# Stacked float32r scores for batch 1, and weights decoded in the tile they land in, in an attention and two-MoE-layer kernel

## The chip, the cores and the metric

One core of one Trainium2 chip runs the whole program; seven cores of the chip are idle. The metric is the device time of one execution in microseconds, the median of several runs. TensorE is called PE here, VectorE DVE, ScalarE ACT, GpSimd POOL, and SyncE, which issues most of the DMAs, SP.

## The reference

The inputs are q, k, v of shape 4 x 8 x 576 x 64 (batch, heads, positions, head size), s of shape 4 x 8 x 576, and five weight matrices that arrive as 64-bit numbers. What is computed, cut to what matters:

```python
scores = scale * q @ k.T
cum = cumsum(maximum(s, 0), axis=-1)
bias = -(cum[:, :, :, None] - cum[:, :, None, :])
scores = where(causal, -1e9, scores + minimum(bias, 0))
x = softmax(scores) @ v            # then 2304 tokens x 512
x = ((x @ w_a) * (x @ w_b)) @ w_out        # 512 -> 1536 -> 512
h = x @ w_in                               # 512 -> 2048
out = (maximum(h, 0) + alpha * minimum(h, 0)) @ w_out2
```

## The kernel before

The 2304 tokens are worked through in five blocks, four of 512 and one of 256. A batch has 576 positions, so block b holds the last 64 positions of batch b-1 and the first 512 (or fewer) of batch b. For each block the two feed-forward layers run on PE (`ffn`, line 1094), and the attention that the next block needs is woven between their matmuls as a list of steps (`attention`, line 895): block 0's matmuls carry the attention of batch 1 (and the tail of batch 0), block 1's that of batch 2, block 2's that of batch 3. The attention of batch 0 comes first, by itself (`first_attention`, line 850). From its pass `i >= FROM_STEPS` on, that lead-in also takes three steps per pass off block 0's list (line 890), six in all: the scores of the tail (`s4`), the scores of heads 0 and 1 of batch 1 for query rows 0 to 255 (`s01`), the next loads, two calls of `both` (biases), and the scores for rows 256 to 383 (`s23`).

The feed-forward layers work in three single-precision products per matrix product: every operand is split into a float32r high part and low part, and `mm3` (lines 1087 to 1089; 1198 to 1200 for the last layer) multiplies high by high, high by low and low by high. A weight tile is 128 x 512; a block uses 68 of them, `NW`, each for 12 matmuls. The split of a weight into `wh` (a copy on ACT) and `wl` (a subtraction on DVE or POOL, line 284) takes place once per block and weight, into six pairs of buffers.

Weights come as 64-bit floats, 512 KB a tile. `load_w` (line 1006) has two ways. The first way loads the 64-bit tile into one of five `raw` tiles (RAW = 5), and `decode` (line 982) turns it into float32: ACT writes the exponent part into `top` (line 987), DVE merges the rest (the SCALAR_TENSOR_TENSOR at line 278). The second way, `again` (line 1038), loads a pair of already decoded tiles from a scratch tensor `w_d` in HBM, 512 KB for two weights. In block 0 every weight goes the first way and is decoded into one of four `w32` tiles; the raw tile is free as soon as the decoding is done. Two thirds of them (46, those whose pair number is not 1 modulo 3) are stored to `w_d` from the w32 tile by a DMA that ACT issues (line 1060); the w32 tile is free when the split and the store are done. The remaining third (22) is not stored in block 0: it is loaded as 64 bits again in block 1, decoded there in place in its raw tile, and stored. From block 2 on all weights come from `w_d`.

Scores (`q_k`, line 494) have two forms. Batches below `STACK` (0 and 1) multiply q and k in plain float32 with a contraction of 64, two heads side by side in the two halves of the array (line 528). Batches 2 and 3 take the stacked form: k is split into high and low parts, q's high and low parts lie one above the other in 128 rows (`stack`, line 435: two copies and two subtractions per head, and two loads of 512 KB per pair of heads instead of two of 256 KB), and each head needs two float32r matmuls with a contraction of 128 (line 502). The stack's tiles kh and qs take two w32 slots each head; `of_stack` opens only when the last weight of block 0 has got its w32 tile.

Biases also have two forms. Batches below `SUMS_PE` (0 and 1) add the running sums on PE, by two float32r matmuls per head and group of rows (lines 518 and 522), and the causal mask comes in with the reduction that moves the scores out of PSUM. For batches 2 and 3 `biases` (line 542) loads each head's running sums to all partitions (`cb`, a broadcast DMA of 256 KB, `load_sums`), forms the bias on DVE or ACT (lines 571 and 575) and masks the diagonal on POOL (line 581).

The order of instructions on each engine is made while the program is built. `Order` holds a rough clock of each engine; every vector operation is placed on the engine that can start or end it first, in order of start and then of due time, where loads of weights have 10 us of slack and splits 5 us. An operation that DVE's second port and POOL share counts as holding both ("port", line 86). DMAs of SP go out in the order of the program, and a DMA that waits for a buffer holds up those behind it. At most ten weights beyond the one in use are asked for (AHEAD = 10, line 1073). The ring of PSUM banks for attention has two banks in the blocks; a step needs both free.

The planner's weave is one line (1232): steps are spread evenly over the block's 272 groups of matmuls.

```python
want = min(len(steps), (i + 1) * len(steps) * FASTER / total)
```

Of the kernel before, what the change touches and what calls it, by code (L numbers as in the profile page):

```python
# [11 lines left out]
I32 = mybir.dt.int32  # L12
# [9 lines left out]
P = 128  # L22
# [33 lines left out]
LATE, LATE_0 = 1000.0, 1300.0  # L56
SL_LOAD, SL_PARTS, SL_QK, SL_BIAS = 10000.0, 5000.0, 5000.0, 2500.0

SUMS_PE = 2

STACK = 2

TURN, SPACE = 1, 5


FROM_WEIGHTS, AHEAD, FROM_LEAD, FROM_STEPS, STEPS = 2, 10, 3, 4, 3


FASTER, BEFORE = 1.06, 6
# [129 lines left out]
def attention_two_moe_kernel(  # L199
# [16 lines left out]
    NW = w64.shape[0]  # L216
    NF1 = (NW - 2 * NF2) // 3
    WN = 512
# [10 lines left out]
    wraw = ctx.enter_context(tc.tile_pool(name="wraw", bufs=1))  # L229
# [6 lines left out]
    W32, RAW, KQ, VB, CB, KL, TOPS = 4, 5, 3, 4, 3, 2, 2  # L236
# [4 lines left out]
    of_raw, of_kq, of_w32, of_w, of_vb, of_t, of_pb, of_c0, of_c1, of_kl = (  # L241
        Slots(n) for n in (RAW, KQ, W32, 6, VB, 4, 1, CB, 2, 0)
    )
    of_stack = Slots(0)

    ctx.enter_context(
        tc.manual_schedule(
# [3 lines left out]
    run = Order()  # L251
# [598 lines left out]
    def first_attention():  # L850
        nonlocal ahead
        s_sb = work.tile([BH, S], F32, name="s_sb", tag="z4")
        nc.scalar.activation(alpha_sb[:, 0:1], ident[:, 0:1], AF.Exp)
        nc.sync.dma_start(s_sb, s)
        for i in range(2):
            load_kq(0, i, 0)
        run.now = 2000.0
        run.pump()
        running_sums(s_sb)
        run.now = 5000.0  # L860
        for rs in ((0, 1), (2,)):
            both(0, 0, rs)
        for i in range(HP + 2):
            if i + 2 < HP:
                load_kq(0, i + 2, 0)
            if i < HP:
                load_v(0, i, 0)
                both(0, i, (3,))
                s01(0, i)
                if i + 1 < HP:  # L870
                    both(0, i + 1, (0, 1))
            if 0 <= i - 2:
                av(0, i - 2, 0)
            if i < HP:
                s23(0, i, 2)
                if i + 1 < HP:
                    both(0, i + 1, (2,))
                s23(0, i, 3)
            if i == FROM_WEIGHTS:
                nc.sync.dma_start(alpha_sb, alpha)  # L880
                ahead = AHEAD
                prefetch()
            if i == FROM_LEAD:
                for f, args in plan[0][0]:
                    f(*args)
            if 0 <= i - 1 < HP:
                for c in range(3):
                    for j in range(2):
                        turn(0, 2 * (i - 1) + j, c)
            if i >= FROM_STEPS:  # L890
                for f, args in plan[0][1][:STEPS]:
                    f(*args)
                del plan[0][1][:STEPS]

    def attention(blk):

# [109 lines left out]
    def load_w(n):  # L1006

        i = n % NW
        postponed = i // 2 % 3 == 1
        new = n < NW or (n < 2 * NW and postponed)  # L1010
        kept = new and postponed == (n >= NW)
        got = []

        def acquire():

            if n:
                yield turns[n - 1]
            yield fetched
            yield of_w

        def first():
            yield of_raw
            r = w64p.tile([P, 2 * WN + 2], I32, name="raw", tag="raw", bufs=RAW)
            yield from dma(r.bitcast(U16)[:, 1:1 + 4 * WN], w64[i].bitcast(U16))
            if n < NW:
                yield of_w32
                w = wraw.tile([P, WN], I32, name="w32", tag="w32", bufs=W32)
                if n == NW - 1:
                    for j in range(2):
                        run.give(of_stack, run.t)  # L1030
            else:
                w = r[:, 0:WN]
            source.append(w)
            yield from decode(n, r, w)
            if n < NW:
                run.give(of_raw, run.t)

        def again():
            if i % 2 == 0:
                pairs[i] = run.spawn(load_pair(i))  # L1040
            yield pairs[i - i % 2]
            source.append(pairs[i - i % 2, "w"][:, i % 2, :])

        def parts():
            yield turns[n]
            h = wsp.tile([P, WN], F32R, name="wh", tag="wh")
            l = wsp.tile([P, WN], F32R, name="wl", tag="wl")
            got.extend((h, l))
            yield from split(f32(source[0]) if new else source[0], h, l)
            if kept:  # L1050
                run.spawn(keep(stored), run.t)
            elif new:
                run.give(of_w32, run.t)
            elif i % 2:
                run.give(of_raw, run.t)

        def store():
            yield fetched
            yield {"act": 330}, 700
            nc.scalar.dma_start(w_d[i].bitcast(I32), source[0])  # L1060
            yield {"dma": P * WN / 90}, 900

        def keep(stored):
            yield stored
            run.give(of_w32 if n < NW else of_raw, run.t)

        source = []
        fetched = run.spawn(first() if new else again(), slack=SL_LOAD)
        stored = run.spawn(store()) if kept else None
        turns[n] = run.spawn(acquire())  # L1070
        return got, run.spawn(parts(), slack=SL_PARTS)

    def prefetch():
# [225 lines left out]
```

## Time and profile before

| | us |
|---|---|
| median of 3 runs | 1002.03 |
| lowest and highest of the runs | 998.98, 1002.17 |
| the profiled execution | 998.65 |
| its span, first to last instruction | 996.9 |
| PE busy in the span | 977.4 |
| DVE, ACT, POOL busy | 699.0, 566.8, 251.2 |
| mean granted TensorE clock | 0.998 |

The span is 1.75 us shorter than the profiled execution's own time. PE's busy time is a union of records whose ends are modelled; the start of one matmul to the start of the next tells more.

### The profile page before, as it was taken

How to read it: one execution, taken by the hardware profiler on the slowest of the kernel's cores; microseconds unless marked ns; L12 is line 12 of the kernel's file. 1: busy time of each engine (PE TensorE's matmuls, PEld its weight loads, DVE VectorE, ACT ScalarE, POOL GpSimd, SP SyncE). 2: the span in 40 equal slices, each digit the busy share in tenths (PEclk: the TensorE clock that was granted, in tenths of full speed). 3: DMA queues.
4: the chain of work that ended last, by engine and by line, in shares of the span. 5: the costliest groups of instructions: out<-in, count | busy, mean ns of one | idle time of the engine just before them, and what ended most of it. 6: DMA issues, size and time to landing. Idle time of an engine off the chain costs nothing.

```text
span 996.9 us, 16282 instructions
## 1 busy us (share of the span) xinstructions
PE 977.4 (98%) x5381; PEld 808.2 (81%) x5381; DVE 699.0 (70%) x1612; ACT 566.8 (57%) x1154; POOL 251.2 (25%) x308
## 2 busy tenths in 40 slices
PE   6989999999999999999999999999999999999998
PEld 5667777778888888788888888888888888889997
DVE  7888877886779788977477777954444474546685
ACT  5866766776655566555554446644433354446664
POOL 2131221441224342432142214522010032210032
PEclk9999999999999999999999999999999999999999
DMA  6599999899688979568387665563542523317551
GB/s 181 188 286 315 349 324 324 295 340 305 237 279 266 317 245 317 192 223 278 103 263 252 188 232 166 185 191 107 190 161 84 171 84 119 132 59 245 185 181 51
DMA packets 149332, 214.62 MB, mean 215 GB/s; under 512 B 36288, under 2 KB 80320, under 8 KB 149248
## 3 DMA queue, kind: packets, MB, share of 16 engines
q1 hardware_dynamic: 139456, 195.76, 61.4%
q10 hardware_dynamic: 9792, 17.83, 4.8%
q8 instruction: 42, 0.69, 0.3%
q14 instruction: 42, 0.34, 0.1%
HBM read 169.95 MB, written 43.59 MB: 214 GB/s over the span
## 4 chain that ended last, share of the span: by engine, by line
PE 91%; DVE 3%; issue 2%; DMA 2%; ACT 1%; POOL 0%; SPq 0%; POOLq 0%; DVEq 0%; ACTq 0%
PE bank L1087 21%; PE bank L1088 21%; PE bank L1089 21%; PE bank L1198 7%; PE bank L1199 6%; PE bank L1200 6%; PE bank L766 2%; PE bank L502 2%; PE bank L706 1%; PE bank L528 1%; PE bank L827 1%; DMA raw<-in_w_dram 1%; DVE z L278 1%; PE bank L518 1%; ACT z L262 0%
## 5 line engine op out<-in xcount | busy, mean ns | idle before, releaser
L1087 PE MATMUL bank<-xh,wh 128*128 128x512 f32 (+1 forms) x800 | 298.6, 373 | 2.3 <-DVE g L278 2.3
L1088 PE MATMUL bank<-xl,wh 128*128 128x512 f32 (+1 forms) x800 | 294.7, 368 | 0.1
L1089 PE MATMUL bank<-xh,wl 128*128 128x512 f32 (+1 forms) x800 | 294.5, 368 | 0.0
L270 ACT ACTIVATE wh<-raw 128x512 fp32r<-128x512 f32 x267 | 166.8, 626 | 106.2 <-PE bank L1088 62.7
L284 POOL TENSOR_TENSOR wl<-raw,wh 128x512 fp32r<-128x512 f32 x83 | 110.5, 1332 | 360.4 <-ACT wh L270 297.3
L284 DVE TENSOR_TENSOR wl<-raw,wh 128x512 fp32r<-128x512 f32 x189 | 132.7, 703 | 92.5 <-ACT wh L270 87.5
L1087 PEld LDWEIGHTS bank<-xh,wh 128*128 128x128 f32 x800 | 150.8, 188 | 32.9 <-issue 4.8
L1088 PEld LDWEIGHTS bank<-xl,wh 128*128 128x128 f32 x800 | 150.8, 189 | 25.5 <-DVE xl L278 0.5
L1089 PEld LDWEIGHTS bank<-xh,wl 128*128 128x128 f32 x800 | 150.8, 188 | 25.4
L270 ACT ACTIVATE gh<-g 128x512 fp32r<-128x512 f32 (+1 forms) x140 | 82.1, 587 | 65.2 <-DVE g L278 62.8
L284 DVE TENSOR_TENSOR gl<-g,gh 128x512 fp32r<-128x512 f32 (+1 forms) x127 | 86.8, 683 | 38.2 <-ACT gh L270 36.2
L1198 PE MATMUL bank<-wh,gh 128*128 128x512 f32 x288 | 113.5, 394 | 0.0
L1199 PE MATMUL bank<-wl,gh 128*128 128x512 f32 x288 | 112.3, 390 | 0.0
L1200 PE MATMUL bank<-wh,gl 128*128 128x512 f32 x288 | 112.1, 389 | 0.0
L262 ACT ACTIVATE z<-z,mn 128x128 f32<-128x128 f32 (+4 forms) x144 | 82.8, 576 | 43.4 <-DVE mn L278 42.2
L1087 PE MATMUL bank<-gh,wh 128*128 128x512 f32 (+1 forms) x240 | 89.7, 374 | 0.0
L1088 PE MATMUL bank<-gl,wh 128*128 128x512 f32 (+1 forms) x240 | 88.7, 370 | 0.3 <-DVE gl L284 0.3
L1089 PE MATMUL bank<-gh,wl 128*128 128x512 f32 (+1 forms) x240 | 88.3, 368 | 0.0
L262 ACT ACTIVATE m<-bank 128x512 f32<-128x512 f32 (+1 forms) x80 | 44.1, 552 | 64.0 <-PE bank L1089 63.6
L987 ACT ACTIVATE top<-raw 128x512 f16<-128x512 bf16 x90 | 69.5, 785 | 17.1 <-DMA raw<-in_w_dram 16.2
L289 DVE TENSOR_SCALAR m<-m,alpha_sb 128x512 f32<-128x512 f32 (+1 forms) x70 | 34.8, 497 | 50.1 <-ACT m L262 49.2
L270 ACT ACTIVATE a_sb<-bank 128x512 f32<-128x512 f32 (+1 forms) x60 | 33.0, 549 | 60.4 <-PE bank L1089 58.5
(91 smaller groups left out, 1397.0 us busy)
## 6 DMA issues: line engine op xcount, KB each, us to landing
raw<-w_d SPq DMA_DIRECT2D x125, 512.0 KB, 4.3
raw<-in_w_dram SPq DMA_DIRECT2D x90, 512.0 KB, 5.8
w_d<-w ACTq DMA_DIRECT2D x46, 256.0 KB, 5.4
zd<-zt SPq DMA_DIRECT2D x48, 192.0 KB, 4.0
pt<-zd SPq DMA_DIRECT2D x48, 192.0 KB, 4.2
kq<-in_kq_a_dram SPq DMA_DIRECT2D x16, 512.0 KB, 6.3
vb<-in_v_dram SPq DMA_DIRECT2D x112, 64.0 KB, 4.1
zd<-zt SPq DMA_DIRECT2D x24, 256.0 KB, 3.6
```

The source lines that it names most:

```text
L262: nc.scalar.activation(o, i, func, **k)
L270: nc.scalar.activation(o, i, AF.Copy, scale=by)
L284: (nc.gpsimd if eng == "pool" else nc.vector).tensor_tensor(o, i0, i1, op=ALU.subtract)
L289: (nc.gpsimd if eng == "pool" else nc.vector).tensor_scalar(o, i, s0, s1, op0=ALU.mult, op1=ALU.mult)
L502: nc.tensor.matmul(d, qs[:, r * P:n], k[:, 0:n], start=i == 0, stop=i == 1)
L987: nc.scalar.activation(top.bitcast(F16).rearrange("p (n t) -> p n t", t=2)[:, :, 1], r.bitcast(BF16)[:, 4:4 + 4 * WN].rearrange("p (n t) - ...
L1087: nc.tensor.matmul(o, wh, ih, start=first, stop=False)
L1088: nc.tensor.matmul(o, wh, il, start=False, stop=False)
L1089: nc.tensor.matmul(o, wl, ih, start=False, stop=last)
L1198: nc.tensor.matmul(acc[t], gh[:, c], wh, start=first, stop=False)
L1199: nc.tensor.matmul(acc[t], gh[:, c], wl, start=False, stop=False)
L1200: nc.tensor.matmul(acc[t], gl[:, c], wh, start=False, stop=last)
```

## The change

Four things change. `SUMS_PE` and `STACK` fall from 2 to 1, so that batch 1 takes the stacked scores and the biases of the vector engines, as batches 2 and 3 do. The lead-in no longer takes six steps off block 0's list. The weights of block 0 are decoded in their raw tile, as the late third was; the raw tile is held until the weight is split and, where it is stored, until the store has landed. And the store is spread: a weight is decoded from 64 bits up to the block that equals its pair number modulo 3 and stored there, so that blocks 0, 1 and 2 (the first three) decode 68, 44 and 22 weights and store 24, 22 and 22. `of_stack` starts with two slots, and w32 tiles now serve the stack alone.

```diff
-SUMS_PE = 2
-STACK = 2
+SUMS_PE = 1
+STACK = 1
...
-FROM_WEIGHTS, AHEAD, FROM_LEAD, FROM_STEPS, STEPS = 2, 10, 3, 4, 3
+FROM_WEIGHTS, AHEAD, FROM_LEAD = 2, 10, 3
...
-    of_stack = Slots(0)
+    of_stack = Slots(2)
...
-            if i >= FROM_STEPS:
-                for f, args in plan[0][1][:STEPS]:
-                    f(*args)
-                del plan[0][1][:STEPS]
...
     def load_w(n):
         i = n % NW
-        postponed = i // 2 % 3 == 1
-        new = n < NW or (n < 2 * NW and postponed)
-        kept = new and postponed == (n >= NW)
+        new, kept = n // NW <= i // 2 % 3, n // NW == i // 2 % 3
...
             yield from dma(r.bitcast(U16)[:, 1:1 + 4 * WN], w64[i].bitcast(U16))
-            if n < NW:
-                yield of_w32
-                w = wraw.tile([P, WN], I32, name="w32", tag="w32", bufs=W32)
-                if n == NW - 1:
-                    for j in range(2):
-                        run.give(of_stack, run.t)
-            else:
-                w = r[:, 0:WN]
-            source.append(w)
-            yield from decode(n, r, w)
-            if n < NW:
-                run.give(of_raw, run.t)
+            source.append(r[:, 0:WN])
+            yield from decode(n, r, source[0])
...
             if kept:
                 run.spawn(keep(stored), run.t)
-            elif new:
-                run.give(of_w32, run.t)
-            elif i % 2:
+            elif new or i % 2:
                 run.give(of_raw, run.t)
...
         def keep(stored):
             yield stored
-            run.give(of_w32 if n < NW else of_raw, run.t)
+            run.give(of_raw, run.t)
```

## Rows read from the trace of the kernel before

**Rows 1.** The page's chain that ended last, by engine.

```profile
PE 91%; DVE 3%; issue 2%; DMA 2%; ACT 1%; POOL 0%; SPq 0%; POOLq 0%; DVEq 0%; ACTq 0%
```

**Rows 2.** Blocks 0, 1, 2: length, then busy us of PE, PEld, DVE, ACT, POOL.

```profile
56.20:275.80 219.60, 217.61 (x1175) 172.97 (x1174) 174.12 (x381) 149.82 (x292) 57.79 (x63) 1.00 0.92 306
275.80:490.50 214.70, 212.37 (x1137) 176.22 (x1136) 168.24 (x392) 124.91 (x257) 70.70 (x87) 1.00 0.77 248
490.50:702.50 212.00, 212.00 (x1137) 176.40 (x1136) 151.50 (x367) 110.23 (x233) 63.29 (x79) 1.00 0.62 196
```

**Rows 3.** Timeline of PE: a matmul ahead of and behind batch 1's scores (start, length).

```profile
79.50 0.39 PE L1089 MATMUL bank<-xh,wl 128*128 128x512 f32 x1
...
81.70 0.39 PE L1089 MATMUL bank<-xh,wl 128*128 128x512 f32 x1
...
112.09 0.39 PE L1089 MATMUL bank<-gh,wl 128*128 128x512 f32 x1
...
114.47 0.40 PE L1089 MATMUL bank<-gh,wl 128*128 128x512 f32 x1
```

**Rows 4.** The same around batch 2's stacked scores, in block 1.

```profile
280.66 0.39 PE L1089 MATMUL bank<-xh,wl 128*128 128x512 f32 x1
...
282.27 0.39 PE L1089 MATMUL bank<-xh,wl 128*128 128x512 f32 x1
...
302.07 0.39 PE L1089 MATMUL bank<-xh,wl 128*128 128x512 f32 x1
...
303.66 0.39 PE L1089 MATMUL bank<-xh,wl 128*128 128x512 f32 x1
```

**Rows 5.** Timeline of PE in the lead-in's last two passes, with idle time and releaser.

```profile
41.56 2.31 PE L773 MATMUL bank<-pt,vb 128*64 128x512 f32 x6
...
46.34 2.40 PE L733 MATMUL bank<-ident,z 128*128 128x128 f32 x20
...
51.68 0.37 PE L528 MATMUL bank<-kq 64*128 64x128 f32 x1 [1.20 <-DMA kq<-in_kq_a_dram]
...
52.76 2.37 PE L773 MATMUL bank<-pt,vb 128*64 128x512 f32 x16
...
58.93 0.97 PE L518 MATMUL bank<-cums,rows 64*128 64x512 f32 x2 [1.72 <-DVE mn L278]
```

**Rows 6.** PE's waits from 60 us on (total, times, longest), its largest.

```profile
PE bank L1087 <- DVE g L278: 2.3, 1, 2.3
```

**Rows 7.** Groups by line and shape over the whole run: the decoding's two operations.

```profile
L987 ACT ACTIVATE top<-raw 128x512 f16<-128x512 bf16 x90 | 69.5, 785 | 17.1 <-DMA raw<-in_w_dram 16.2 <-DMA cb<-cum_d 0.5
...
L278 DVE SCALAR_TENSOR_TENSOR raw<-raw,top 128x512 int32<-128x512 int32 x22 | 16.2, 750 | 3.4 <-ACT top L987 3.4
```

**Rows 8.** The busiest stretch of 40 us in block 1 (columns as in Rows 2).

```profile
396.00:436.00 40.00, 37.67 (x217) 31.08 (x216) 33.55 (x85) 25.15 (x55) 16.95 (x22) 1.00 0.67 217
```

**Rows 9.** Groups: the softmax scaling on DVE in two widths, and POOL's diagonal mask.

```profile
L289 DVE TENSOR_SCALAR z<-z,sm 128x512 f32<-128x512 f32 x28 | 16.4, 606 | 0.5
...
L289 DVE TENSOR_SCALAR z<-z,sm 128x128 f32<-128x128 f32 x20 | 10.0, 511 | 0.2
...
L581 POOL TENSOR_SCALAR_AFFINE_SELECT z<-z 128x256 f32<-128x256 f32 x16 | 9.9, 635 | 13.0 <-DVE z L571 10.5 <-ACT z L575 2.4
```

**Rows 10.** SP's own waits from 60 to 271 us: total, times, longest.

```profile
SPq L295 <- DVE w L278: 21.9, 18, 3.8
```

**Rows 11.** SP's timeline in block 0: the first and the last of nine raw loads.

```profile
184.55 1.50 SPq L295 DMA_DIRECT2D raw<-in_w_dram  x2
...
211.22 6.17 SPq L295 DMA_DIRECT2D raw<-in_w_dram  x4
```

**Rows 12.** Groups by line and shape: the two operations of a weight's split.

```profile
L270 ACT ACTIVATE wh<-w 128x512 fp32r<-128x512 f32 x67 | 41.6, 628 | 25.0 <-DVE w L278 9.1 <-PE bank L1088 5.0 <-PE bank L1089 2.3
...
L284 POOL TENSOR_TENSOR wl<-w,wh 128x512 fp32r<-128x512 f32 x31 | 41.2, 1329 | 100.2 <-ACT wh L270 58.3 <-DVE g L278 20.4 <-DVE m L289 8.0
```

**Rows 13.** DMA issues from 60 to 271 us: stores of block 0 (KB, us to landing).

```profile
w_d<-w ACTq DMA_DIRECT2D x43, 256.0 KB, 5.5
```

## The prediction, written before the change was run

> **What bounds the kernel now.** I read the chain of waits first: 91% of it is PE [rows 1], so time comes off where PE does less or waits less. The table of busy times by block says how much room the other engines have [rows 2]: in block 0 PE is busy 217.6 of 219.6 us, DVE 174.1 (79%), ACT 149.8 (68%), POOL 57.8; in block 1 DVE 168.2 of 214.7 (78%), ACT 124.9. DVE is the next engine. PE's timeline shows batch 1's scores between feed-forward matmuls [rows 3] and batch 2's stacked scores in block 1 [rows 4]; there the reader measures from the start of one matmul to the start of another, since the ends are modelled. The lead-in shows where PE waits today [rows 5], and PE's waits show that after 60 us there is only one of weight, 2.3 us for a DVE result in block 1 [rows 6].
>
> **The change, part by part.**
>
> *Scores.* For two heads, query rows 0 to 255: from the matmul ahead to the third one behind took 81.70 - 79.50 = 2.20 us in the old form [rows 3] and 282.27 - 280.66 = 1.61 us in the stacked form [rows 4], 0.59 us less. For query rows 384 to 511: 2.38 against 1.59, 0.79 less. The group between (query rows 256 to 383) I take at the mean, 0.69. So 2.07 us per pair of heads, and four pairs: 8.3 us of PE's time, on the path. Bounds: all groups like the smaller, 3 x 4 x 0.59 = 7.1; all like the larger, 9.5. Those numbers hold the sums' matmuls and the switching between forms, because the stretch ends at ordinary matmuls.
>
> *The six steps moved out of the lead-in.* Their matmuls are still done, in block 0. With them go two waits: 1.20 us for a kq load and 1.72 us for a reduction that had to free a bank [rows 5]. But they stood between the last transposes and the last attention product of the lead-in, whose input is copied out of PSUM by ACT in that time. How long that takes uncovered is shown one pass earlier: the product ran from 41.56 to 46.34, 4.78 us, where the covered one took 2.37 [rows 5], so 2.4 us come back. Net -0.5; bounds -2.9 (ACT copies in time) and +1.9 (the 2.4 come back, half of the two old waits remain or recur as a wait for weights: 2.4 - 0.5; nothing in the trace excludes that). SP has the moved loads later in its queue, behind weights; I cost that at nothing, covered by the matmuls between one step and the next; without that cover it is another wait of 1.2 us.
>
> *Vector work of block 0.* After the change block 0 is what block 1 is today, with 68 decodings in place of 22. That gives its load without guessing at each stack and bias: 46 decodings at 0.750 us on DVE and 0.785 us on ACT [rows 7] on top of block 1's rows [rows 2]: DVE 168.2 + 34.5 = 203 us, ACT 124.9 + 36.1 = 161 us, in a block that PE would finish in 219.6 - 8.3 = 211 us. DVE at 96% is too much to be left there; the planner gives a subtraction to whichever of DVE and POOL starts first, and POOL has two thirds of its time free. Today's busiest 40 us of block 1 (DVE 33.55, 84%) hold the one stall of 2.3 us [rows 6, 8]. Blocks above that load should have more. For block 0 I take one; none is the lower end; one in each of five stretches of 40 us, 11.7 us, the upper.
>
> *Blocks 1 and 2.* Each gets 22 more decodings: DVE +16.5, ACT +17.3 us, so block 1 stands at 185 of 215 us (86%), block 2 at 168 of 212 (79%). Block 2 then is where block 1 is now. For both together I take half a stall more, 1.2 us; bounds -2.3 (the present one is not met again) and +4.7 (two).
>
> *DMA.* Block 0 drops 22 stores (5.6 MB) and gains eight broadcasts and larger kq loads (4.1 MB); block 2 gains 22 stores where DMA is 62% busy [rows 2]. Nothing on the path, and covered by the weights' lead; without it, see the raw tiles below.
>
> **Sum.** -8.3 - 0.5 + 2.3 + 1.2 = -5.3 us. The profiled execution took 998.65 us (span 996.9, 1.75 around it), 3.4 below the median of 1002.03. I set the difference against the median: 996.7 us. A measurement of this kernel can tell about 0.3%, 3 us, from no change.
>
> **The rivals.**
>
> *The vector engines become the bound (no gain).* For it: DVE at 203 of 211 us, and POOL as an outlet that costs DVE time. The softmax scaling of 128 columns takes 511 ns on DVE, that of 512 columns 606 [rows 9]: a quarter of the work at 84% of the time, so much of the short one must be waiting, and it has no input that another engine could still owe it. The eight heads of batch 1 add masks on POOL, some 0.635 us for the first two row groups alone [rows 9], 5.1 us for eight heads. The Trainium skill (SBUF — State Buffer, "Who interferes with whom") says that DVE and GpSimd share a port pair as an exclusive lock, held for a whole instruction while the other engine fully blocks; by that rule each mask and each subtraction moved to POOL takes its length from DVE, and the two rows agree with it. Against it: there is no PE wait in block 0 at 79%, and decodings and splits can be late, the softmax not. Price: five stalls of 2.3 in block 0 and two in block 1 in place of my one and a half, +12.6 -> 1009 at its worst; half of that, the likelier depth, gives 1003.
>
> *Five raw tiles become the bound (slower).* Place: block 0. Today a raw tile is free when it is decoded, and even so SP stood 18 times, 21.9 us, waiting for just that [rows 10]. Between 184.55 and 211.22 us eight loads went out (two at the first row, six between), one per 3.33 us [rows 11], so that each of five tiles came round in 16.7 us. The change holds it longer: by the split, 0.63 + 1.33 us [rows 12] with POOL doing the subtraction, or, in 24 of 68, by the store's 5.5 us [rows 13]. That is 44/68 x 2.0 + 24/68 x 5.5 = 3.2 us, 19.9 us a round, 4.0 us a weight, against 211/68 = 3.1 that PE asks for. If this holds in half of the block, 34 weights are 0.9 us late each, 31 us; six pairs of split weights cover up to 6 x 3.1 = 19 us; 12 us reach PE. From 996.7 that is 1009. It decides where a round takes more than 5 x 3.1 = 15.5 us. Against it: the 16.7 contains waits of a queue that was well ahead, and SP's waits moved no PE time; and the planner, which sees the longer hold, orders the decoding accordingly.
>
> *Nothing else is late (faster still).* POOL takes enough of DVE's work, and the only stall of today is not met again: -8.3 - 0.5 - 2.3 gives 991. For it: the late work is all of the kind that can wait, and the rest of block 1 runs at 78% of DVE without a stall. Against it: its busiest stretch stalled at 84% [rows 6, 8], and block 0 will be above that on the mean.
>
> That the stacked form waits for its own preparation (copies and subtractions that begin only when the pair before is through) is a smaller one: at 1.2 us per pair, as the kq wait, it would add 4.8 and give 1001.5. In block 1 those matmuls stand in rows without idle time [rows 4], so I give it little.
>
> **How the numbers follow.** Forecast (one to two new stalls) 0.45; the vector engines 0.22; the raw tiles 0.20; nothing late 0.10; late stacks 0.03. Of the forecast, 0.40 lies beyond 3 us on the fast side and 0.05 within; of the vector case 0.14 within, 0.06 slower, 0.02 faster; of the raw tiles 0.17 slower, 0.03 within; nothing late is faster, late stacks are within. Faster 0.52, same 0.25, slower 0.23. The range runs from 989 (nothing late, and the lead-in at its lower end, 991 - 2.4) to 1010, the raw tiles in half of block 0 with an uncertain microsecond; about one in ten lies outside on the slow side, where the whole block would be held up, and less than that on the other. The likeliest case by itself: 993 to 1000.
>
> **What would show it.** The scores of batch 1 as L502-like rows at 0.9, 0.7 and 0.9 us per pair, in block 0; no wait for kq in the lead-in, and an attention product of some 4.8 us ahead of the first feed-forward matmul; 134 decodings; block 0 shorter by 5 to 8 us, blocks 1 and 2 longer by 0 to 3, and blocks 3 and 4 the same. DVE above 88% in block 0, with PE's waits naming g or mn. Wrong would be: PE waiting for wl or wh in block 0, and SP waiting for the store or the split ahead of raw loads (raw tiles); PE's waits above 10 us in blocks 0 and 1 with DVE named (vector engines); a block 0 that is no shorter although no wait shows, which would mean that the stacked form costs more there than in block 1.

## The result, and the profile after

The changed kernel takes 1010.07 us (median of 6 runs, 1008.51 to 1015.48) against 1001.9 for the kernel before beside it (6 runs): ratio 1.0093, 95% interval 1.0066 to 1.0119. It is 8.2 us slower where 5.3 us less were forecast. The profiled execution took 1008.51, with a span of 1006.7, 9.8 more than before.

First the page's chain that ended last, by engine [rows 1 before], and one of its groups [rows 7]:

```profile
PE 71%; DMA 12%; DVE 6%; issue 5%; ACT 3%; POOL 1%; SPq 1%; ACTq 0%; POOLq 0%; DVEq 0%
...
L983 ACT ACTIVATE top<-raw 128x512 f16<-128x512 bf16 x134 | 103.6, 786 | 55.3 <-DMA raw<-in_w_dram 53.5
```

PE has fallen from 91% to 71% of the chain, and DMA has risen from 2 to 12%. ACT's decoding, 134 times in place of 90, was idle 53.5 us for raw loads (16.2 before [rows 7]). Then the busy times by block, with the columns of [rows 2]; the row of a block begins at its first feed-forward matmul and ends at that of the next:

```profile
50.40:282.70 232.30, 219.97 (x1138) 177.68 (x1138) 185.45 (x412) 169.42 (x337) 73.62 (x92) 0.99 0.87 289
282.70:496.00 213.30, 212.75 (x1138) 176.08 (x1137) 178.22 (x407) 138.78 (x280) 81.96 (x90) 1.00 0.85 280
496.00:712.40 216.40, 214.09 (x1138) 177.49 (x1136) 163.71 (x384) 120.87 (x249) 71.42 (x86) 0.99 0.73 240
```

So the lead-in ends 5.8 us earlier (50.4 against 56.2), block 0 is 12.8 us longer (232.3 against 219.5), block 1 is 1.4 shorter, block 2 is 4.4 longer, and blocks 3 and 4 are unchanged at 192.9 and 97.6. But for rounding, that adds up to the span's +9.8. The DMA engines had no more to move: in block 0 they were busy 0.92 of the time at 306 GB/s before [rows 2], and 0.87 at 289 now. PE is idle 12.3 us of block 0 (2.0 before [rows 2]), while DVE has 47 us free. PE's waits from 50.4 us on, the largest (in total, times, longest):

```profile
PE bank L1071 <- DVE wl L284: 3.4, 2, 3.0
PE bank L1180 <- ACT gh L270: 3.3, 2, 2.2
PE bank L502 <- DVE mn L278: 2.3, 2, 1.8
PE bank L1069 <- ACT wh L270: 1.7, 2, 1.3
```

Weights are waited for (wl, wh), and with them gh, which ACT makes in program order behind the decoding; the two waits for mn lie in blocks 1 and 2. What the loads waited for is in SP's own waits in block 0:

```profile
SPq L295 <- DMA w_d<-raw: 41.3, 15, 6.0
SPq L295 <- DMA raw<-in_w_dram: 17.4, 18, 3.3
...
SPq L295 <- DVE wl L284: 14.5, 12, 5.1
```

Stores hold SP for 41.3 us, and splits (wl) for 14.5. SP waited for stores in the kernel before as well, in its block 0:

```profile
SPq L295 <- DMA w_d<-w: 24.6, 16, 4.9
```

One piece of the chain of waits shows how that reaches PE (start, length, what):

```profile
257.37 5.81 DMA raw<-in_w_dram
...
263.26 0.80 ACT top L983
...
266.64 0.65 DVE raw L278
...
267.32 5.15 DMA w_d<-raw
...
272.52 3.94 DMA raw<-in_w_dram
...
276.54 0.79 ACT top L983
...
277.96 0.70 DVE gl L284
...
278.70 0.76 PE bank L1182
```

A raw tile is decoded and its store takes 5.15 us. Only then does SP load the next weight; ACT's next decoding stands waiting for that, and what is queued behind it is late: gh, then gl, then the matmul. Taken over the weights 12 to 67 of block 0, from the records of the traces: a raw load was issued 16.0 us after its weight was asked for (4.3 before), counted from the first matmul of the weight ten places ahead of it, and a split was ready 4.0 us before its matmul (12.3 before). Two thirds of the lead are gone.

The stacked scores did what they should. PE's timeline in block 0, one matmul ahead of each of the three groups of a pair of heads and the third one behind it [rows 3, 4]:

```profile
195.93 0.39 PE L1071 MATMUL bank<-xh,wl 128*128 128x512 f32 x1
...
197.54 0.39 PE L1182 MATMUL bank<-wh,gl 128*128 128x512 f32 x1
...
204.35 0.39 PE L1182 MATMUL bank<-wh,gl 128*128 128x512 f32 x1
...
205.76 0.39 PE L1182 MATMUL bank<-wh,gl 128*128 128x512 f32 x1
...
219.80 0.39 PE L1182 MATMUL bank<-wh,gl 128*128 128x512 f32 x1
...
221.38 0.39 PE L1071 MATMUL bank<-xh,wl 128*128 128x512 f32 x1
```

1.61, 1.41 and 1.58 us, where the kernel before took 2.20, 2.07 and 2.38: 2.05 per pair, 8.2 in all four if they are alike. (This is the fourth pair; the first two took 1.99 and 1.88 us for their first group.)

### The profile page after: what moved, and what is told of

The parts are those of the page before. It is cut to its first block, busy times and chain, and to the rows that moved or that the text cites. A ratio compares the mean times of both kernels' runs of the same rounds, so it can differ in the third digit from the quotient of the medians.

```text
span 1006.7 us, 16432 instructions
## 1 busy us (share of the span) xinstructions
PE 977.1 (97%) x5317; PEld 809.6 (80%) x5317; DVE 732.3 (73%) x1666; ACT 610.4 (61%) x1240; POOL 286.4 (28%) x344
## 4 chain that ended last, share of the span: by engine, by line
PE 71%; DMA 12%; DVE 6%; issue 5%; ACT 3%; POOL 1%; SPq 1%; ACTq 0%; POOLq 0%; DVEq 0%
PE bank L1069 16%; PE bank L1070 16%; PE bank L1071 16%; PE bank L1182 5%; PE bank L1180 5%; PE bank L1181 5%; DMA raw<-in_w_dram 5%; DMA zd<-zt 3%; DMA w_d<-raw 2%; PE bank L502 2%; PE bank L766 2%; DMA cb<-cum_d 1%; PE bank L706 1%; ACT z L262 1%; DVE raw L278 1%
## 5 line engine op out<-in xcount | busy, mean ns | idle before, releaser
L284 POOL TENSOR_TENSOR wl<-raw,wh 128x512 fp32r<-128x512 f32 x121 | 161.7, 1340 | 395.3 <-ACT wh L270 303.4
L270 ACT ACTIVATE wh<-raw 128x512 fp32r<-128x512 f32 x335 | 207.9, 625 | 108.0 <-PE bank L1070 44.5
L284 DVE TENSOR_TENSOR wl<-raw,wh 128x512 fp32r<-128x512 f32 x219 | 152.5, 698 | 90.3 <-ACT wh L270 84.5
L983 ACT ACTIVATE top<-raw 128x512 f16<-128x512 bf16 x134 | 103.6, 786 | 55.3 <-DMA raw<-in_w_dram 53.5
L278 DVE SCALAR_TENSOR_TENSOR raw<-raw,top 128x512 int32<-128x512 int32 x134 | 98.6, 746 | 27.7 <-ACT top L983 24.5
L581 POOL TENSOR_SCALAR_AFFINE_SELECT z<-z 128x128 f32<-128x128 f32 (+2 forms) x104 | 53.3, 520 | 140.8 <-DVE z L571 81.7
L262 ACT ACTIVATE m<-bank 128x512 f32<-128x512 f32 (+1 forms) x80 | 43.9, 548 | 51.9 <-PE bank L1071 50.5
```

The source lines that it names most:

```text
L262: nc.scalar.activation(o, i, func, **k)
L270: nc.scalar.activation(o, i, AF.Copy, scale=by)
L278: f(*args, **k)
L284: (nc.gpsimd if eng == "pool" else nc.vector).tensor_tensor(o, i0, i1, op=ALU.subtract)
L581: nc.gpsimd.affine_select(d, d, pattern=pattern, base=0, channel_multiplier=1, compare_op=ALU.is_ge, fill=MASKED,)
L983: nc.scalar.activation(top.bitcast(F16).rearrange("p (n t) -> p n t", t=2)[:, :, 1], r.bitcast(BF16)[:, 4:4 + 4 * WN].rearrange("p (n t) - ...
```

## The experiments

Labels are shortened in the text to their first part. "Start" is the time of block 0's first feed-forward matmul, the end of the lead-in. Lengths are those of the profiled execution, from a block's first feed-forward matmul to the next block's, and to the last matmul for block 4. Each ratio is against runs of the kernel before beside it. "Stores" counts the weights stored in blocks 0 to 3. Each kernel is the changed one with the edit named; from `e13` on, `top` is taken from a list of free tiles instead of by the weight's number. `e2`, `e3`, `e4`, `e6` and `e11` give another output than the reference, with as many operations and transfers. The likely reason is that two decodings which are open at once can get the same `top`, so that a weight is merged with another's exponent part; `e14`, with the list and all stores in block 3, has blocks 0 to 2 within 0.6 us of those of `e11`.

| run | median us | ratio to before, 95% | start | block 0 | 1 | 2 | 3 | 4 | stores |
|---|---|---|---|---|---|---|---|---|---|
| before | 1001.9 | | 56.2 | 219.5 | 214.7 | 212.0 | 192.9 | 97.6 | 46, 22, 0, 0 |
| after | 1010.07 | 1.0066 to 1.0119 | 50.4 | 232.3 | 213.3 | 216.4 | 192.9 | 97.6 | 24, 22, 22, 0 |
| e1 | 1010.87 | 1.0036 to 1.0095 | 52.3 | 229.6 | 217.4 | 217.0 | 192.9 | 97.6 | 24, 22, 22, 0 |
| e2 | 1015.21 | 1.0095 to 1.0192 | 49.6 | 219.4 | 233.9 | 214.7 | 192.9 | 97.7 | 0, 24, 22, 22 |
| e3 | 1008.03 | 1.0042 to 1.0086 | 52.5 | 231.0 | 213.2 | 214.4 | 192.9 | 97.6 | as after |
| e4 | 1016.35 | 1.0103 to 1.0178 | 56.3 | 230.9 | 214.1 | 216.0 | 192.9 | 97.7 | as after |
| e5 | 1017.57 | one run | 53.3 | 235.4 | 214.4 | 218.4 | 192.9 | 97.6 | as after |
| e6 | 1020.51 | 1.0142 to 1.0205 | 53.4 | 234.9 | 224.6 | 212.4 | 192.9 | 97.6 | as after |
| e7 | 1027.36 | 1.0230 to 1.0293 | 51.4 | 243.4 | 216.1 | 217.3 | 192.9 | 97.6 | as after |
| e7b | 1042.63 | 1.0378 to 1.0429 | 50.5 | 248.1 | 236.1 | 212.4 | 192.9 | 97.7 | as after |
| e8 | 1031.24 | 1.0277 to 1.0331 | 51.5 | 221.0 | 223.1 | 215.0 | 194.7 | 122.5 | none |
| e9 | 1026.57 | 1.0219 to 1.0283 | 52.8 | 249.7 | 216.3 | 212.0 | 192.9 | 97.6 | 68, 0, 0, 0 |
| e10 | 1012.70 | 1.0075 to 1.0169 | 52.8 | 234.5 | 214.4 | 215.9 | 192.9 | 97.6 | as after |
| e11 | 1010.24 | 1.0072 to 1.0122 | 50.5 | 217.9 | 215.5 | 212.2 | 193.0 | 115.3 | none |
| e13 | 1014.22 | 1.0092 to 1.0154 | 53.1 | 225.7 | 222.6 | 214.7 | 192.9 | 97.6 | as after |
| e14 | 1002.63 | 0.9990 to 1.0029 | 50.3 | 217.4 | 215.5 | 212.2 | 203.4 | 97.6 | 0, 0, 0, 68 |
| e15 | 1013.88 | 1.0097 to 1.0149 | 50.1 | 216.0 | 219.5 | 230.5 | 192.9 | 97.6 | 0, 0, 34, 34 |
| e17 | 1013.56 | 1.0087 to 1.0160 | 50.0 | 220.1 | 221.0 | 216.4 | 200.9 | 97.6 | 0, 0, 0, 68 |
| e18 | 999.44 | 0.9962 to 1.0004 | 53.0 | 218.0 | 215.5 | 212.2 | 194.1 | 100.2 | 0, 0, 0, 34 |
| e19 | 1007.47 | 1.0039 to 1.0087 | 55.1 | 218.0 | 215.5 | 217.6 | 194.5 | 100.2 | 0, 0, 0, 34 |

**Which part of the change?** The kernel before with the weights' part alone (`load_w` and `of_stack` as in the change, scores and lead-in as before).

> The kernel before with only the weights' part of the change (decoded in the raw tile, a third stored in each of the first three blocks); scores, biases and lead-in as before. Raw tiles as the cause: block 0 takes 226 to 236 us instead of 219.5, PE waits there for wl or wh, the run 1007 to 1016 us. Vector engines as the cause: block 0 has no stack and no biases of batch 1, so it stays within 3 us of 219.5, and the run at 1000 to 1004.

The weights' part by itself makes the kernel slower, by a ratio of 1.0066 where the whole change has 1.0093. Its block 0 is 10 us longer than before, without one stacked score of batch 1. But PE's waits there don't name wl or wh, as was expected: the longest is 2.9 us for ovl, the others are for g, gh and gl, and its splits were ready 11.2 us before their matmul. ACT's waits in that block, and the chain ahead of the wait for ovl, show the late loads all the same:

```profile
ACT top L987 <- DMA raw<-in_w_dram: 40.7, 31, 4.1
...
101.95 6.82 DMA raw<-in_w_dram
...
108.86 0.78 ACT top L987
...
109.67 0.69 DVE raw L278
110.36 0.54 DVE xl L284
...
110.92 0.23 ACT ovh L270
...
111.18 0.24 DVE ovl L284
```

ACT stood 40.7 us for raw loads (8.9 before, 27.2 after), and what came behind the decoding in the order of DVE and ACT (xl, ovh, ovl) was late with it. So a late load can reach PE without a late weight. And beside the weights' part the rest of the change brought next to nothing: 1010.87 us without it and 1010.07 with it, although PE is busy 984.0 us in the one and 977.1 in the other.

The six steps put back into the lead-in of the changed kernel:

> The changed kernel with the six steps of block 0's list back in the lead-in. Block 0 starts 4 to 6 us later (at 54 to 57 us) and is 2.6 us shorter for the matmuls that left it. If the six steps' vector work is what overfills block 0, it is 8 us or more shorter and the run comes to 1000 to 1005; if the weights' tiles are, the run stays at 1007 to 1014.

The lead-in ends at 56.3, as before, and block 0 is still 230.9 us long: the moved steps are not what made it long. The whole, 1016.35, lies above both ranges.

**The store or the decoding?** Every store one block later:

```diff
-        new, kept = n // NW <= i // 2 % 3, n // NW == i // 2 % 3
+        new, kept = n // NW <= i // 2 % 3 + 1, n // NW == i // 2 % 3 + 1
```

> The changed kernel with every third stored one block later (none in block 0, a third in each of the next three; 68 more decodings in blocks 1 to 3). Raw tiles as the cause: with no store to wait for in block 0 it falls from 232 to 213 to 221 us and PE waits there under 4 us; blocks 1 to 3 grow by 0 to 8 us in all. Vector engines as the cause: block 0 has the same vector work and stays at 228 or above.

Block 0 decodes its 68 weights as it did, and is 12.9 us shorter; block 1, which now decodes 68 and stores 24, is 20.6 longer (blocks 1 to 3 were to grow by 0 to 8 in all). Then no store at all (`new, kept = True, False`), and all 68 in block 0 (`n < NW, n < NW`):

> The changed kernel with no store at all: every block loads all 68 weights in raw form and decodes them again. Theory (a raw tile that is held until its store has landed makes the next load late): block 0 as in the run without its stores, 219.4 us; blocks 1 and 2, with 68 decodes but no hold, 213 to 217 each; blocks 3 and 4 within 3 us of 192.9 and 97.6; in all 50.4 + 219.4 + 215 + 214 + 195 + 99 + 5.6 behind the last block's start sum = 998. Rival (the decoding itself, 0.79 us of ScalarE and 0.75 us of VectorE for each weight, in line with the rest): block 0 about 219, but blocks 1 and 2 at 225 to 234, like the 233.9 of the block that decoded 68 and stored 24, and block 3 longer as well: about 1030.

> The changed kernel with all 68 weights stored from their raw tiles in block 0 in place of 24; blocks 1 and 2 then decode nothing. Theory of the store's hold: 0 stores gave a block 0 of 219.4 us and 24 gave 232.3, so 0.54 us each and 256 us with 68; blocks 1 and 2 at about 212; in all 50.4 + 256 + 212 + 212 + 192.9 + 97.6 + 5.6 = 1026.5. Rival (block 0 is long by its 68 decodes and the stacked scores, the stores count little): block 0 stays at 230 to 236, and the whole comes to 1002 to 1006, since blocks 1 and 2 lose their decodes.

Without stores block 0 took 221.0, and with 68 of them 249.7: 0.42 us for each. The whole met 1026.5 with 1026.57, though block 0 was 6 us below what was expected and block 1 was 4 above. The total of `e8` was the rival's 1030, but not for the rival's reason: its blocks 0 to 3 add up to 853.8 us, where the changed kernel's are 854.9, and the surplus is block 4, 24.9 us longer with 68 raw loads of its own, which neither theory had thought of; block 1, at 223.1, is nearer to the rival's 225 to 234 than to the theory's 213 to 217, and block 2 is at 215.0. So 68 decodings in raw tiles cost block 1 some ten microseconds without any store; `e11` below, with tiles of their own for them, takes 215.5 there.

**Vector work, the planner's clock, more buffers.** Three rivals. Batch 1's rows 0 to 511 without POOL's mask and without the division by the softmax's sum (it leaves out those two):

> The changed kernel, where batch 1's rows 0 to 511 leave out the causal mask on POOL and the softmax's division (some 12 us of POOL and 13 us of DVE or POOL less in block 0; the output lacks them). Vector engines as the cause: block 0 falls to 213 to 220 us. Raw tiles as the cause: it stays at 226 to 233, since every load still waits for the store or the split.

Block 0 is no shorter (235.4), with DVE busy for 178.7 us and POOL for 55.7 (185.45 and 73.6 after): neither the vector load nor POOL's masks decide. That was also where the Trainium skill (SBUF — State Buffer, "Who interferes with whom") would have had its lock between DVE and GpSimd bite; the page has it only for DVE instructions that use the shared ports, which the prediction left out. The trace of the kernel before agrees with a lock: of its twenty scalings of 128 columns [rows 9], the eight with POOL idle took 0.27 us on the mean, the twelve beside a POOL instruction 0.67. But no run here shows that it cost PE anything. The planner told that a weight's load lands 2.2 us and its store 2.4 us later than it assumed:

> The changed kernel, the planner alone altered: it counts a load of a 64-bit weight and a store of a decoded one as landing 2.2 and 2.4 us later than it did, near the 5.7 and 5.1 us that the trace shows. Planned order as the cause (SP and ACT, which work in order, stand behind transfers that land later than planned): PE's wait in block 0 falls from 12.2 us to under 5, block 0 from 232 to 216 to 223 us, the run to 996 to 1002 us. Too few raw tiles as the cause, whatever the order: block 0 stays at 229 to 236.

In block 0 ACT's waits for raw loads fell from 27.2 to 8.2 us, and the block took 234.9. So ACT's waits for loads, as the planner had placed them, are not by themselves what makes the block long. A sixth raw tile, paid for with one of the six pairs of split weights:

> The changed kernel with six raw tiles and five pairs of split weights instead of five and six (the memory is the same). Raw tiles as the cause: a sixth more loads in flight, block 0 at 214 to 223 us, the run at 994 to 1003. Vector engines as the cause: nothing changes for them, block 0 at 229 to 236 us, the run at 1007 to 1013.

231.0, 1.3 us shorter; whether the lost pair takes back what the sixth tile gives is not shown. A tile for decoded weights, so that the raw tile is free at once (four raw and two such, then five and two with a kq tile less):

```diff
...
-            source.append(r[:, 0:WN])
+            yield of_wd
+            source.append(wraw.tile([P, WN], I32, name="wd", tag="wd", bufs=2))
             yield from decode(n, r, source[0])
+            run.give(of_raw, run.t)
...
```

> The changed kernel with four raw tiles and two tiles of their own for decoded weights (the memory is the same): the raw tile is free when it is decoded, as in the kernel before; the small tile is held for split and store. Long hold of the raw tile as the cause: requests for loads wait some 5 us instead of 16, block 0 at 215 to 223 us, the run at 995 to 1003. Planned order or the store's wait as such: the two small tiles are held as long by the store, block 0 at 226 or above.

> The changed kernel with five raw tiles and two more tiles for decoded weights, so that a raw tile is free at its decode and the store holds one of the two; the room comes from the third kq tile. Theory (the number of tiles between load and split is what sets block 0): seven tiles against the five of the changed kernel and the nine of the kernel before, so block 0 between 219.5 and 232.3, about 225, and the whole about 1001; the earlier run with four and two had a 243.4 because six tiles are no more than five where the two are held by a store of 5 us. Rival (the late work is in the order of the vector engines' instructions, not in the tiles): block 0 at 230 or longer and the whole 1008 or more. Two kq tiles in place of three may cost waits for L502 that name kq; then the gain is smaller and the trace shows them.

Both theories fell: block 0 took 243.4 and 234.5, as the rivals had it. With 24 stores in block 0 the two new tiles are held (DVE waited 9.1 us for stores before it could write one in `e10`), and SP's waits for stores in `e10` were still 33.7 us; 4.5 us of PE's waits there were for kq_b, the price of the third kq tile. The first of the two with the planner's later landings as well was slower again, 1042.63 (1.0378 to 1.0429), with 248.1 us in block 0:

> Both of the other two edits together. If either cause is the whole of it, as good as the better of the two within 3 us; if both hold a part, better than each, block 0 at 213 to 218 us and the run at 992 to 998.

**The tile, or the transfer?** The stores read from another array, so that they hold no tile:

```diff
-            if kept:
-                run.spawn(keep(stored), run.t)
-            elif new or i % 2:
+            if new or i % 2:
...
-            nc.scalar.dma_start(w_d[i].bitcast(I32), source[0])
+            nc.scalar.dma_start(w_d[i], kq_a[i % B, i % H, :, 0:WN])
```

> The changed kernel, with each of its stores reading 256 KB from another array in memory (kq_a) in place of the decoded tile: as many stores, as large, from the same queue, but a raw tile is free once it is split. It leaves out the weights' own copy, so blocks 1 to 4 compute with other numbers. Theory (the store counts by the tile that it holds): block 0 at 219 to 222 us, as with no stores (219.4 and 221.0), and the whole at 996 to 1000. Rival (the store counts by its traffic or its place in ScalarE's order): block 0 stays at 229 to 235 and the whole at 1007 to 1012.

Between the two theories: block 0 is 225.7, with 7.7 us of idle PE (12.3 after, 3.9 in `e2`). Taking the hold away gives back 6.6 of the 12.9 us that taking the store away gives. SP's own waits in block 0, of `e13`:

```profile
SPq L295 <- DMA w_d<-in_kq_a_dram: 26.1, 11, 4.5
SPq L295 <- DVE wl L284: 24.4, 19, 3.4
SPq L295 <- DMA raw<-in_w_dram: 15.1, 14, 2.7
```

and of `e2`, without stores there:

```profile
SPq L295 <- DVE wl L284: 30.8, 17, 5.0
...
SPq L295 <- DMA raw<-in_w_dram: 4.7, 9, 0.9
```

SP waits 26.1 us for stores whose tiles it never writes. (Of the 41.3 us after, 16.3 stood directly before a raw load for the tile itself, six times.) The trace has the reason: all DMA issues, SP's and ACT's, take eight completion semaphores in turn (94 or 95 issues each after), and in the kernels before, after and `e13` no issue came before the previous transfer of its semaphore had landed, so that at most eight were in flight. The Trainium skill (DMA: Bandwidth & Descriptors, "Why a DMA increments its semaphore by 16 and not by 1") asks for one semaphore per transfer in flight; by that rule eight allow eight, and the trace agrees. So a store of 5 to 6 us takes one of eight places, and the loads behind it queue in SP's order. In block 0, SP's waits for its own semaphore came to 53.6 us after, 52.4 in `e13`, 16.0 in `e2`; the kernel before had 48.5 and 46 stores, beside its lead of 12.3 us. In `e10` they came to 63.5, and all of its 33.7 us for stores were for such a place: two more tiles do nothing for that part. The whole of `e13`, 1014.22, was worse than either theory, because of block 1 (222.6): one wait of 4.8 us for g, at 413 us, behind some ten microseconds of DVE's own work in line, and a lower clock beside it, 3.4 us. So block 1 lost 9.3 us where block 0 won 6.6, and the half that the hold seems to cost rests on this one pair of kernels.

**Where can the stores go?** No store, with five raw and two decoded tiles and two kq tiles; the same with all stores in block 3; with half in block 2 and half in 3; and all in block 3 held in the raw tiles:

```diff
-        new, kept = n // NW <= i // 2 % 3, n // NW == i // 2 % 3
+        new, kept = n // NW <= 3, n // NW == 3                                    # e14, e17
+        new, kept = n // NW <= 2 + i // 2 % 2, n // NW == 2 + i // 2 % 2          # e15
+        new, kept = n // NW <= 3 or i // 2 % 2 == 1, n // NW == 3 and i // 2 % 2 == 0   # e18
```

> Both: no store at all, five raw tiles, two tiles for decoded weights, two kq tiles. Theory: the two causes of a late load are gone, so block 0 comes below the 219.4 of the run without its stores, at 214 to 218, blocks 1 and 2 at 213 to 215, and the whole at 990 to 996, faster than the kernel before. Rival (decodes in line on ScalarE and VectorE): blocks 1 and 2 at 220 or more, and the whole over 1005.

> Five raw tiles, two tiles for decoded weights, two kq tiles, every weight decoded anew in blocks 0 to 3, and all 68 stored in block 3, which has only the last attention beside it; block 4 loads the stored copies. Theory of the hold: blocks 0 to 2 as in the run with no store, 217.9, 215.5 and 212.2 us; block 3 with 68 stores at 193 to 197, because VectorE and ScalarE have little else to do there; block 4 back from 115.3 to 97.6; in all 1010.2 - 17.7 + 0 to 4 = 992.5 to 996.5, faster than both kernels. Rival (a store costs its 0.5 us in any block): block 3 at 193 + 68 x 0.5 = 227 and the whole at 1026.

> The same with half of the stores in block 2 and half in block 3. Theory: block 2, with 34 stores beside batch 3's attention, grows by 34 x 0.5 = 17 us if it is like block 0, to about 229, or by less where it has more slack (212.2 without stores, no PE wait): 212 to 220; the whole between 993 and 1003, not better than all stores in block 3. Rival (the hold matters only beside batch 1's attention): block 2 stays at 212 and the whole is the same as with all in block 3, within 1 us.

> All 68 stored in block 3, but held in the five raw tiles as in the changed kernel, with three kq tiles and no tile for decoded weights. Theory: blocks 0 to 2 as in the run with no store on raw tiles, 221.0, 223.1 and 215.0 us; block 3 at 195 to 200; block 4 at 97.6; in all 1031.2 - 24.9 + 0 to 5 = 1006 to 1011. The distance to the run with two own tiles, some 14 us, is then what the hold from decode to split costs without any store. Rival (a store costs 0.5 us in any block): block 3 at 228 and the whole at 1039.

Blocks 0 to 2 of `e11` came within a microsecond of what was expected; block 4 took 17.7 us more, as it took 24.9 more in `e8`, and the whole missed its 990 to 996. Blocks 0 to 2 of `e14` repeat them, and block 4 is back at 97.6; but block 3 grew by 10.4, not by 0 to 4, and so the whole is level with the kernel before. `e15` puts 34 stores into block 2, and that block grows by 18.3, 0.54 us each, while 34 stores in block 3, beside 34 decodings, cost nothing (192.9); its whole, 1013.88, missed 993 to 1003. `e17` is 11 us slower than `e14`, its raw tiles being held until the split, five tiles in place of seven: blocks 0 to 2 take 12.5 us more.

So half of the stores, in block 3, and the other half of the weights decoded to the end; and the same with the scores' part undone:

> As the run with all stores in block 3 (1002.6 us; its block 3 took 203.4 for the 193.0 without stores), but only every other pair is stored there, 34 weights, and block 4 decodes the other 34 anew. Theory: blocks 0 to 2 as there, 217.4, 215.5 and 212.2; block 3 loses half of its 10.4 or more, 194 to 199; block 4, which needed 115.3 when it decoded all 68 and 97.6 when it decoded none, 98 to 103; in all 996 to 1001, below the kernel before. Rival (the last block is short of transfer time as soon as it loads raw weights): block 4 at 106, half way, and the whole at 1003 to 1006.

> The same with the scores' part of the change undone: batch 1's running sums on the PE, its products not stacked, the six steps back in the lead-in. Theory (the sum of the prediction was right for this part and only the late weights hid it): 8 to 9 us longer than the same kernel with stacked scores: the lead-in ends at 56 in place of 50, block 0 at 218 to 222, and the whole at 1005 to 1009. Rival (the stacked scores are paid back by their vector work wherever they stand): the two are within 3 us.

Blocks 0, 2, 3 of `e18` (columns as above):

```profile
53.00:271.00 218.00, 213.99 (x1138) 176.19 (x1137) 188.89 (x409) 173.52 (x344) 82.08 (x97) 1.00 0.85 285
...
486.50:698.70 212.20, 212.20 (x1137) 176.45 (x1136) 189.85 (x432) 153.92 (x301) 73.71 (x82) 1.00 0.85 284
698.70:892.80 194.10, 193.17 (x913) 158.57 (x912) 137.94 (x241) 123.97 (x206) 27.27 (x32) 1.00 0.77 252
```

and blocks 0 and 2 of `e19`:

```profile
55.10:273.10 218.00, 217.40 (x1175) 172.99 (x1174) 175.88 (x389) 151.02 (x288) 52.01 (x57) 1.00 0.81 263
...
488.60:706.20 217.60, 214.20 (x1138) 177.44 (x1137) 193.66 (x440) 151.91 (x296) 73.35 (x79) 0.99 0.84 276
```

`e18` takes 999.44 us, ratio 0.9983 with an interval from 0.9962 to 1.0004: 1.1% below the changed kernel by the two ratios, and not told apart from the kernel before. Undoing the scores adds 8.0 us, as expected. But the rows say that not all of this is PE's work. PE is busy 3.4 us less in block 0 with stacked scores, although it does the six steps too; there 3.4 us more of waits took that back, and the lead-in ends 2.0 earlier. The largest piece, 5.4 us in block 2, is two waits for weights in `e19`, 3.4 us, and slower matmuls after them, in a block whose scores the part does not touch. Whether they belong to it is open; without them the scores and the steps are worth 2.4 us here.

## Why the prediction was wrong

*The scores* (-8.3): right as PE's work, 2.05 us per pair, and over the whole run PE is busy 7.7 us less in `e18` than in `e19`. That it comes off the time is not shown: `e1` is level with the changed kernel, and of the 8.0 us between `e18` and `e19` 5.4 lie in block 2. *The six steps* (-0.5, bounds -2.9 and +1.9): not shown. The two waits went, but they are gone from `e1` too, which keeps the steps and starts block 0 at 52.3; and the second of them stood in block 0 already (58.93 us [rows 5], where the block begins at 56.2). Of the 5.8 us by which the lead-in ended earlier, 1.7 are clock: its granted clock averaged 0.97 before and 1.00 after. The last attention product took 3.7 us (46.68 to 50.40) where 4.8 was expected, and part of the rest is the first pair's scores that moved with the steps.

*Vector work of block 0* (+2.3): the wrong engine. DVE was forecast at 203 us; it was busy 185.45, and 188.9 in `e18`. It was ACT that took most of the rest (169.4 us for the 161 forecast): all 36 biases were formed there (line 575), where block 1 before, from which the 203 was worked out, had formed 27 of its 36 on DVE (line 571, 10.7 us). POOL took 73.6 us for that block's 70.7. `e5` took vector work away and block 0 did not shrink. *Blocks 1 and 2* (+1.2, bounds -2.3 and +4.7): +3.0, in the bounds.

**The step that failed is the one on DMA**: "Nothing on the path, and covered by the weights' lead". The price of the lost cover stood only with the rival of five raw tiles, at 0.20, and the argument against that rival, "SP's waits moved no PE time", was the error: in the kernel before they moved none beside nine tiles, five raw and four w32, and a lead of 12.3 us. The change took the four away. In their place the runs show late raw loads: they were issued 16.0 us after their weight was asked for (4.3 before), the lead fell to 4.0 us, and without its 24 stores block 0 is 12.9 us shorter (`e2`). PE's idle time in block 0 rose by 10.3 us, and the lower clock after the long waits took 3.4 more; 3.6 us of PE's work were saved against that (217.6 busy before, 214.0 in `e18`, at the full clock), and the remaining 2.6 us of block 0's +12.8 are in small pieces.

The rival gave 1009 us and 12 us at PE; measured were 1010.07 and 12.3. What it named as proof, PE waiting for wl and wh and SP for the store and the split, is what the profile shows. Yet its sum was right partly by luck: it counted the hold alone, which `e13`, if its block 0 is taken by itself, puts at about half of the store's cost, and knew neither the eight transfer places nor the clock. How the other half divides between those places, the transfer's own traffic and ACT's order is not settled. Nor is all of `e10`, where more tiles gave nothing, nor how the lead and the loss go together: `e1` had a lead of 11.2 us and a block 0 of 229.6, `e14` a lead of 7.9 and one of 217.4. Comparisons of one block between two kernels also carry up to some 9 us of the planner's new order and the clock (block 1 of `e13`, block 2 of `e19`). What rests on families carries less of that: block 0 with no stores took 216.0 to 221.0 in eight kernels (`e19`, with the old scores, among them), and with 24 held ones in raw tiles 229.6 to 235.4 in six (`e1` among them).

## What to carry to other kernels

A wait that costs nothing today is paid for by a lead somewhere; before a change takes buffers, work out that lead and what is left of it. The lead alone doesn't decide, though: look also at what stands behind a late load in the order of each engine (`e1`). A buffer's life is the unit: from the issue of its load to the last thing that reads it, a store's landing included. And put stores that only later stages need into the stage with the most slack: the same 34 stores cost 18 us beside batch 3's attention in block 2, and 0 and 1.1 in block 3 (all 68 there cost 10.4).

## What the runs showed of the hardware

A wait can cost more than its length. PE's timeline in the changed kernel, after the longest wait for a weight:

```profile
185.67 0.50 PE L1071 MATMUL bank<-xh,wl 128*128 128x512 f32 x1 [3.02 <-DVE wl L284]
...
187.65 0.63 PE L1071 MATMUL bank<-xh,wl 128*128 128x512 f32 x1
188.08 0.63 PE L1069 MATMUL bank<-xh,wh 128*128 128x512 f32 x1
...
190.60 0.39 PE L1181 MATMUL bank<-wl,gh 128*128 128x512 f32 x1
190.82 0.39 PE L1182 MATMUL bank<-wh,gl 128*128 128x512 f32 x1
```

and the stretch behind it, with the columns of [rows 2]:

```profile
187.00:190.50 3.50, 3.50 (x10) 2.73 (x10) 1.61 (x4) 1.61 (x4) 0.00 (x0) 0.57 0.94 229
```

From 187 to 190 us matmuls begin 0.43 us apart in place of 0.22: 1.2 GHz instead of 2.4, with a granted clock of 0.57 over the stretch. A wait of 2.2 us near 278 us is followed by the same (0.60 from 279 to 283). In block 0 the granted clock averaged 0.985, which is 3.4 us of 232.3; in `e9`, whose PE was idle for 19.2 us of block 0, 0.945, or 13.7 us. But the clock did not fall after every such wait. Behind the 2.3 us wait of [rows 6], which ended at 404.3 us, and behind one of 3.0 us in `e2`, which ended at 471.7, it stayed at 1.00. Here is the stretch behind the first:

```profile
404.30:408.30 4.00, 3.98 (x17) 3.30 (x18) 3.62 (x8) 2.90 (x5) 1.11 (x2) 1.00 0.90 319
```

In the lead-in PE waits 5.7 us for DVE (cum) in every run, and the clock falls near 21 us in the kernel before, `e18` and `e19`, but not after, nor in `e1` and `e14`. So a difference of 1.7 us between two runs' starts can be the clock alone.
